# Joining maxima and sums over four partition groups: six VectorE copies in place of a TensorE transpose

## The chip, the cores and the metric

The kernel runs on one core of one Trainium2 chip. The metric is the device time of one execution in microseconds; lower is better. Before the change the median of 3 runs is 2840.31 us (2839.74 to 2840.36). A core has five engines that run their own instruction streams and meet at semaphores: TensorE (PE in the profile, with its weight loads as PEld), VectorE (DVE), ScalarE (ACT), GpSimd (POOL) and SyncE (SP), which issues most transfers. SBUF is the memory that all of them work on; TensorE writes its results to PSUM.

## The reference

One transformer block on 2048 rows of width 576: a modulated layer norm, attention against a cache (32 query heads on 16 key/value heads of width 128, the last 512 keys), and a gated MLP of width 4608. Everything is fp32.

```python
mod = (silu(c) @ w_mod)            # sa, ca, ga, sb, cb, gb
h = layernorm(x) * (1 + ca) + sa
q = (h @ wq)                       # 32 heads of 128
scores = einsum("bhqd,bhkd->bhqk", q, k[last 512]) * 128 ** -0.5
p = softmax(scores)
x = x + ga * (einsum("bhqk,bhkd->bhqd", p, v) @ wo)
h = layernorm(x) * (1 + cb) + sb
x = x + gb * ((relu(h @ W_gate) * (h @ W_up)) @ W_down)
```

## The kernel before

The attention stage runs from about 30 to 1593 us. It is cut into 128 units; a unit u is one query head on one block of 512 queries, against all 512 keys. After it comes the MLP, which the change does not touch. An fp32 product is made of three matmuls: each operand is split into hi (a rounded copy, made by ScalarE) and lo (the rest, made by GpSimd or VectorE), and hi x hi, lo x hi and hi x lo are added up in PSUM.

The order of the work on TensorE, VectorE, ScalarE and GpSimd is written by hand: each engine runs its instructions in the order in which the code issues them. The main loop issues, for unit u:

- the scores s (L541 to L543, 12 matmuls), with keys on partitions and queries along the free axis, and on VectorE t (L546): the maximum over each group of 32 keys, made by a reduction that transposes blocks of 32 x 32;
- `max_pre` (L551): the maximum over the four key tiles, into columns 0 to 15 of the tile mxs. In mxs, partition 32g + j and column b hold the maximum of query 32b + j over the 32 keys of partition group g;
- `sum_pre` (L556): the same for the sums of the unit before, out of its tile ks, into columns 16 to 31;
- `turn` and `spread`: the four partition groups have to be joined. VectorE writes mxs four times over, transposed by blocks of 32, into mt (L562), and TensorE transposes mt into PSUM as qm (L565), after the projection of the next unit (qps, L465, 14 matmuls). Then every partition holds the values of all four groups side by side;
- `max_bc`: VectorE takes the maximum of the four (r, L585), the sum of the four for the unit before (ri, L572), spreads the maxima back along the keys (mb, L589) and inverts the sums (L575);
- p (L602): s - mb on VectorE in two halves, with exp (L604) and hi (L597) on ScalarE; rb (L580), the spread inverse sums; qlo (L523), the low part of the next unit's q, which the next scores need; ks, the sum of the exponentials over the key tiles, begun on VectorE (L619) and finished on GpSimd (L622, two instructions);
- on TensorE the value products pv (L631 to L634) of the unit before and two pieces of the output projection (wo, L687);
- lo (L611) on GpSimd, two halves of 1024 elements, and olo (L676), the low part of an earlier unit's output. Weight splits (L217) for coming units are placed between them.

Scores have two PSUM buffers (psS); projections, qm and pv take turns in two others (psM).

Of the kernel before, what the change touches and what calls it, by code (L numbers as in the profile page):

```python
# [7 lines left out]
F32 = mybir.dt.float32  # L8
# [3 lines left out]
ALU = mybir.AluOpType  # L12
AX = mybir.AxisListType

P = 128
# [11 lines left out]
SUM, MLP0 = 3, 8  # L27
# [4 lines left out]
def kernel(  # L32
# [13 lines left out]
    nc = tc.nc  # L46
# [3 lines left out]
    cp = ctx.enter_context(tc.tile_pool(name="cp", bufs=1))  # L50
# [7 lines left out]
    op = ctx.enter_context(tc.tile_pool(name="op", bufs=3))  # L58
    xp = ctx.enter_context(tc.tile_pool(name="xp", bufs=3))
    sp = ctx.enter_context(tc.tile_pool(name="sp", bufs=2))  # L60
# [4 lines left out]
    psM = psM_scope.__enter__()  # L65
# [3 lines left out]
    ident = cp.tile([P, P], F32, name="ident")  # L69
# [6 lines left out]
    ones = cp.tile([P, P], F32, name="ones")  # L76
    nc.vector.memset(ones, 1.0)

    mxs = cp.tile([P, 32], F32, name="mxs")
    nc.vector.memset(mxs, 0.0)  # L80

    zeros = cp.tile([P, 32], F32, name="zeros")
    nc.vector.memset(zeros, 0.0)
# [217 lines left out]
    def flush(q=None):  # L301
        q = pend if q is None else q
        while q:
            q.pop()()
# [185 lines left out]
    NU = HKV * NQB * 2  # L490
# [17 lines left out]
    def qproj(u, lo, hi):  # L508
        g, qb, h = unit(u)
        if lo == 0:  # L510
            assert ready[qb] == "a"
            ps = psM.tile([P, 512], F32, tag="mm", name=f"qps{u}")
            qst[u] = ps, proj_ops(ps, wqs[h], hT[qb], u)
        for f in qst[u][1][lo:hi]:
            f()

    def q_hi(u):
        qhi[u] = qp.tile([P, 512], F32R, tag="qhi", name=f"qhi{u}")
        nc.scalar.activation(qhi[u], qst[u][0], AF.Copy, bias=0.0, scale=SCALE)  # L519

    def q_lo(u):
        qlo[u] = qp.tile([P, 512], F32R, tag="qlo", name=f"qlo{u}")
        nc.vector.scalar_tensor_tensor(qlo[u], qst.pop(u)[0], SCALE, qhi[u].bitcast(F32),  # L523
                                       op0=ALU.mult, op1=ALU.subtract)

    st_, t4, mt, pt, hi_, lo_, bc, rb, rinv, ks_, pvps, done, o, bps = ({} for _ in range(14))

    def by_sum(u):
        return 0 <= u < SUM
# [3 lines left out]
    def s_half(u, h):  # L533
        g, qb, hd = unit(u)
        k = ks[g]
        t = psS.tile([P, 2, 512], F32, tag="s", name=f"s{u}_{h}")
        st_[u, h] = t
        for j in range(2):
            kt = 2 * h + j
            ps = t[:, j, :]  # L540
            nc.tensor.matmul(ps, k[:, kt, :], qhi[u], start=True, stop=False)  # L541
            nc.tensor.matmul(ps, k[:, 4 + kt, :], qhi[u], start=False, stop=False)  # L542
            nc.tensor.matmul(ps, k[:, kt, :], qlo[u], start=False, stop=True)  # L543
        if h == 0:
            t4[u] = sp.tile([P, 4, 16], F32, tag="t4", name=f"t4_{u}", bufs=1)
        nc.vector.tensor_reduce(t4[u][:, 2 * h:2 * h + 2, :].rearrange("p k b -> p (k b)"),  # L546
                                t.rearrange("p k (b j) -> p (k b) j", j=32),
                                axis=AX.X, op=ALU.max, apply_transpose=True)

    def max_pre(u):  # L550
        nc.vector.tensor_reduce(mxs[:, :16], t4.pop(u).rearrange("p k b -> p b k"), axis=AX.X, op=ALU.max)  # L551

    def sum_pre(u):
        if by_sum(u):
            return
        nc.vector.tensor_reduce(mxs[:, 16:], ks_.pop(u).rearrange("p (b j) -> p b j", j=32),  # L556
                                axis=AX.X, op=ALU.add, apply_transpose=True)

    def turn(u):
        bps[u] = psM.tile([P, 512], F32, tag="mm", name=f"qm{u}")  # L560
        mt[u] = sp.tile([P, P], F32, tag="mt", name=f"mt{u}", bufs=1)
        nc.vector.transpose(mt[u].rearrange("p (a b) -> p a b", a=4), mxs[:, None, :].to_broadcast([P, 4, 32]))  # L562

    def spread(u):
        nc.tensor.transpose(bps[u][:, :P], mt.pop(u), ident)  # L565

    def quads(u, k):
        return bps[u][:, :P].rearrange("p (a k b) -> p k b a", a=4, k=2)[:, k]

    def sum_add(u):  # L570
        r = rinv[u] = sp.tile([P, 16], F32, tag="ri", name=f"ri{u}", bufs=1)
        nc.vector.tensor_reduce(r, quads(u + 1, 1), axis=AX.X, op=ALU.add)  # L572

    def sum_inv(u):
        nc.vector.reciprocal(rinv[u], rinv[u])  # L575

    def sum_bc(u):
        r = rinv.pop(u)
        rb[u] = bp.tile([P, 512], F32, tag="bc", name=f"rb{u}")
        nc.vector.transpose(rb[u].rearrange("p (b j) -> p b j", j=32),  # L580
                            r[:, :, None].to_broadcast([P, 16, 32]))

    def max_bc(u):
        r = sp.tile([P, 16], F32, tag="r", name=f"r{u}", bufs=1)
        nc.vector.tensor_reduce(r, quads(u, 0), axis=AX.X, op=ALU.max)  # L585
        if u > SUM:
            sum_add(u - 1)
        m = bp.tile([P, 512], F32, tag="bc", name=f"mb{u}")
        nc.vector.transpose(m.rearrange("p (b j) -> p b j", j=32),  # L589
                            r[:, :, None].to_broadcast([P, 16, 32]))  # L590
        if u > SUM:
            sum_inv(u - 1)
        bc[u] = m

    def hi_half(u, h):
        hi_[u, h] = pp.tile([P, 2, 512], F32R, tag="hi", name=f"hi{u}_{h}")
        nc.scalar.copy(hi_[u, h], pt[u, h])  # L597
# [11 lines left out]
    def lo_half(u, h):  # L609
        lo_[u, h] = pp.tile([P, 2, 512], F32R, tag="lo", name=f"lo{u}_{h}", bufs=2)  # L610
        nc.gpsimd.tensor_sub(lo_[u, h], pt[u, h], hi_[u, h].bitcast(F32))  # L611
# [54 lines left out]
    def o_mul(u):  # L666
        o[u] = rb.pop(u)
        nc.vector.tensor_tensor(o[u], done.pop(u), o[u], op=ALU.mult)

    def o_hi(u):  # L670
        ohi[u] = op.tile([P, 512], F32R, tag="ohi", name=f"ohi{u}")
        nc.scalar.copy(ohi[u], o[u])

    def o_lo(u):
        olo[u] = op.tile([P, 512], F32R, tag="olo", name=f"olo{u}")
        nc.gpsimd.tensor_sub(olo[u], o.pop(u), ohi[u].bitcast(F32))  # L676
# [45 lines left out]
    def piece(n):  # L722
        add = wo_piece(*pieces[n][1:], seed=seeds.get(n))

        def end():
            add()
            put_seed(n + 1)

        (pend_act if n in seeds else pend).append(end)
        return n in seeds  # L730
# [944 lines left out]
    mlp = mlp_slots()  # L1675

    def last_unit():
        spread(NU)
        sum_add(NU - 1)
        sum_inv(NU - 1)  # L1680
        sum_bc(NU - 1)
        o_mul(NU - 1)
# [67 lines left out]
    def run(u, k):  # L1750
        t = 10 * u + k
        while sched and sched[-1][0] <= t:
            fn, args = sched.pop()[2:]
            fn(*args)
# [11 lines left out]
    for u in range(NU):  # L1766
        run(u, 0)
        if u > 1 and u % 2 == 0:
            o_hi(u - 2)
            o_lo(u - 2)  # L1770
        s_half(u, 0)
        s_half(u, 1)
        max_pre(u)
        if u:
            sum_pre(u - 1)
        turn(u)
        run(u, 1)
        if u + 1 < NU:
            qproj(u + 1, 0, 14)
        else:  # L1780
            piece(at[10 * u + 1])
        if u == 1:
            hi_half(0, 0)
            hi_half(0, 1)
            lo_half(0, 0)
            lo_half(0, 1)
        run(u, 2)
        if u + 1 == NU:
            pv_half(u - 1, 0, True)
        spread(u)  # L1790
        max_bc(u)
        if u + 1 < NU:
            q_hi(u + 1)
        run(u, 3)
        if 10 * u + 3 in at:
            piece(at[10 * u + 3])
        if u > 1 and u % 2:
            o_hi(u - 2)
            o_lo(u - 2)
        run(u, 4)  # L1800
        if by_sum(u - 1):
            pv_sums(u - 1)
        elif u + 1 == NU:
            pv_half(u - 1, 1, True)
        elif u:
            pv_half(u - 1, 0)
        flush(pend_act)
        exp_half(u, 0)
        flush()
        run(u, 5)  # L1810
        if u == 0:
            q_lo(1)
        exp_half(u, 1)
        if u > SUM:
            sum_bc(u - 1)
        if 0 < u < NU - 1:
            q_lo(u + 1)
        if by_sum(u - 1):
            sums_inv(u - 1)
        ksum_op(u, 0)  # L1820
        ksum_op(u, 1)
        run(u, 6)
        if SUM < u < NU - 1:
            pv_half(u - 1, 1)
        if 10 * u + 6 in at:
            piece(at[10 * u + 6])
        run(u, 7)
        if u:
            o_mul(u - 1)
        flush()  # L1830
        run(u, 8)
        if u + 1 == NU:
            flush(pend_act)
        if u:
            hi_half(u, 1)
        flush(pend_act)
        if u:
            lo_half(u, 0)
            lo_half(u, 1)
        run(u, 9)  # L1840
# [56 lines left out]
```

## Time and profile before

| what | before |
|---|---|
| median of 3 runs | 2840.31 us |
| the profiled execution, span of its core | 2839.2 us, 1.1 us under the median of the runs |
| TensorE busy | 2823.0 us (99%) |
| VectorE busy | 2194.6 us (77%) |
| ScalarE busy | 1431.0 us (50%) |
| GpSimd busy | 2206.1 us (78%) |
| granted TensorE clock | 1.000 |

A row of the profile names the engine, the line of the kernel, the operation, the tile written and the tiles read, their shapes and the count. In a list by time the first number is the start in us and the second the duration of the row's instructions together; what stands in brackets is how long the engine was idle before it and which instruction ended that. An instruction's record begins when its engine takes it up, so a wait inside the instruction is part of its duration.

### The profile page before, as it was taken

What the parts mean: (1) busy time and instruction counts of PE and PEld (TensorE: products, weight loads), DVE (VectorE), ACT (ScalarE), POOL (GpSimd) and SP (SyncE); (2) the same over time, 40 slices, a digit from 0 to 9 for tenths busy, and PEclk for the clock granted to TensorE, in tenths of its full rate; (3) what the DMA queues carried; (4) which work ended last, traced back from release to release, by engine and by line L of the source; (5) the groups of instructions that cost most, each with busy time, mean ns of one, the idle gap of its engine ahead of it and who ended that gap; (6) DMA issues with size and microseconds to landing.
All of it is one profiled execution on the core that took longest, in us unless ns stands there. A gap on an engine that the chain in (4) does not pass through costs nothing.

```text
span 2839.2 us, 41692 instructions
## 1 busy us (share of the span) xinstructions
PE 2823.0 (99%) x15183; PEld 2457.3 (87%) x15183; DVE 2194.6 (77%) x3220; ACT 1431.0 (50%) x2020; POOL 2206.1 (78%) x1596
## 2 busy tenths in 40 slices
PE   9999999999999999999999999999999999999999
PEld 7888888888888888888888888888888888888888
DVE  8988788888888888777988877787787566666666
ACT  6766666676666666666756433333333222222220
POOL 6878888888898988777788766778888577777773
PEclk9999999999999999999999999999999999999999
DMA  6322122223332223322244465666677844444443
GB/s 248 109 76 97 60 94 95 84 70 109 106 96 85 93 67 132 100 69 86 73 144 136 149 219 203 228 228 232 248 254 281 313 154 155 156 156 154 152 149 136
DMA packets 166876, 411.40 MB, mean 145 GB/s; under 512 B 15728, under 2 KB 62576, under 8 KB 166672
## 3 DMA queue, kind: packets, MB, share of 16 engines
q1 hardware_dynamic: 132768, 287.65, 31.4%
q10 hardware_dynamic: 33904, 121.09, 10.9%
q8 instruction: 120, 1.97, 0.3%
q14 instruction: 84, 0.69, 0.1%
HBM read 276.53 MB, written 160.73 MB: 154 GB/s over the span
## 4 chain that ended last, share of the span: by engine, by line
PE 90%; POOL 4%; DVE 2%; ACT 2%; issue 1%; DMA 1%; ACTq 0%; SPq 0%; POOLq 0%; DVEq 0%
PE gh_P L1163 28%; PE wo L687 12%; PE qps L465 12%; PE md L687 9%; PE mf L771 6%; PE s L543 4%; PE s L542 4%; PE s L541 3%; PE pv L634 3%; PE pv L632 3%; PE pv L631 3%; POOL lo L611 2%; PE gu L1163 1%; POOL ks L622 1%; ACT p L604 1%
## 5 line engine op out<-in xcount | busy, mean ns | idle before, releaser
L611 POOL TENSOR_TENSOR lo<-p,hi 128x1024 fp32r<-128x1024 f32 x256 | 610.1, 2405 | 0.5
L622 POOL TENSOR_TENSOR ks<-ks,p 128x512 f32<-128x512 f32 x250 | 334.5, 1338 | 247.5 <-ACT p L604 203.4
L546 DVE TRANSPOSE_TENSOR_REDUCE t<-s 128x32 f32<-128x1024 f32 x256 | 317.6, 1245 | 137.9 <-PE s L543 125.6
L1163 PE MATMUL gh_P<-hop_B,wop 128*128 128x512 f32 x1470 | 352.9, 390 | 0.6 <-issue 0.6
L1163 PEld LDWEIGHTS gh_P<-hop_B,wop 128*128 128x128 f32 x1470 | 270.0, 188 | 51.2 <-DVE q L1200 0.8
L602 DVE TENSOR_TENSOR p<-s,mb 128x1024 f32<-128x1024 f32 x256 | 299.9, 1209 | 0.3
L465 PE MATMUL qps<-hTa,wA 128*128 128x512 f32 x1176 | 282.6, 391 | 0.7 <-DVE hTa L447 0.3
L1163 PE MATMUL gh_P<-hop_T,wop 128*128 128x512 f32 x1138 | 282.8, 390 | 0.0
L687 PE MATMUL wo<-woga,ohi 128*128 128x288 f32 x1344 | 279.1, 300 | 1.0 <-POOL woga L217 0.5
L604 ACT ACTIVATE p<-p 128x1024 f32<-128x1024 f32 x256 | 270.4, 1056 | 17.4 <-DVE p L602 17.4
L597 ACT CAST hi<-p 128x1024 fp32r<-128x1024 f32 x256 | 268.9, 1051 | 6.9
L465 PEld LDWEIGHTS qps<-hTa,wA 128*128 128x128 f32 x1176 | 220.1, 188 | 47.9 <-DVE hTa L447 0.8
L687 PE MATMUL md<-wogb,hhi 128*128 128x288 f32 x1280 | 257.2, 294 | 0.0
L519 ACT ACTIVATE qhi<-qps 128x512 fp32r<-128x512 f32 x128 | 76.6, 598 | 337.2 <-PE qps L465 337.2
L1163 PEld LDWEIGHTS gh_P<-hop_T,wop 128*128 128x128 f32 x1138 | 208.8, 188 | 39.3
L687 PEld LDWEIGHTS wo<-woga,ohi 128*128 128x128 f32 x1344 | 218.7, 188 | 16.2 <-ACT p L604 0.8
L687 PEld LDWEIGHTS md<-wogb,hhi 128*128 128x128 f32 x1280 | 212.3, 188 | 10.5 <-DVE q L1188 0.2
L698 DVE TENSOR_TENSOR acc<-md,acc 128x576 f32<-128x576 f32 x160 | 120.0, 754 | 107.2 <-PE md L687 106.1
L1163 PE MATMUL gh_P<-hy_T,wop 128*128 128x512 f32 x618 | 200.6, 391 | 0.0
L687 PE MATMUL wo<-woga,olo 128*128 128x288 f32 x672 | 198.8, 296 | 1.2 <-POOL olo L676 1.1
L687 PE MATMUL md<-wogb,hlo 128*128 128x288 f32 x640 | 188.8, 295 | 0.0
L696 ACT COPY acc<-wo 128x576 f32<-128x576 f32 x228 | 145.0, 636 | 55.1 <-PE wo L687 50.5
(322 smaller groups left out, 7279.7 us busy)
## 6 DMA issues: line engine op xcount, KB each, us to landing
wop<-wk_P SPq DMA_DIRECT2D x133, 640.0 KB
wk_P<-wop ACTq DMA_DIRECT2D x119, 640.0 KB
wr<-wlay SPq DMA_DIRECT2D x68, 384.0 KB
againq<-akq SPq DMA_DIRECT2D x22, 640.0 KB
againo<-ako SPq DMA_DIRECT2D x18, 576.0 KB
rogb<-wd SPq DMA_DIRECT2D x36, 288.0 KB
rwA<-wq SPq DMA_DIRECT2D x32, 320.0 KB
roga<-wo SPq DMA_DIRECT2D x32, 288.0 KB
```

The lines of the kernel that those rows point to most:

```text
L465: return [lambda i=i, a=a, b=b: nc.tensor.matmul(ps, a, b, start=(i == 0), stop=(i == n - 1)) for i, (a, b) in enumerate(ops)]
L546: nc.vector.tensor_reduce(t4[u][:, 2 * h:2 * h + 2, :].rearrange("p k b -> p (k b)"), t.rearrange("p k (b j) -> p (k b) j", j=32), axis=AX ...
L597: nc.scalar.copy(hi_[u, h], pt[u, h])
L602: nc.vector.tensor_tensor(p, t, bc[u][:, None, :].to_broadcast([P, 2, 512]), op=ALU.subtract)
L604: nc.scalar.activation(p, p, AF.Exp, bias=0.0, scale=1.0)
L611: nc.gpsimd.tensor_sub(lo_[u, h], pt[u, h], hi_[u, h].bitcast(F32))
L622: nc.gpsimd.tensor_tensor(ks_[u], ks_[u], p[:, j, :], op=ALU.add)
L687: nc.tensor.matmul(ps[:, half, :H2], a[:, sl], w[b][:, cs], start=(n == 0 and seed is None), stop=(n == 5), skip_group_check=seed is not None)
L696: nc.scalar.copy(av, ps[:, :, :H2])
L698: nc.vector.tensor_tensor(av, ps[:, :, :H2], av, op=ALU.add)
L771: nc.tensor.matmul(ps[:, j, :H2], x[:, sl], w[:, c:c + H2], start=i == 0, stop=i == 2)
L1163: nc.tensor.matmul(ps, a, c, start=s not in ("P2", "P3") and i == 0, stop=i == len(ops) - 1, skip_group_check=True)
```

## The change

The tile mxs gets a second axis of four. After max_pre and sum_pre, three VectorE copies bring the 32 columns of partition groups 1, 2 and 3 beside those of group 0, on partitions 0 to 31. Two reductions there take the maximum and the sum of the four, into the tile both, and three copies bring the result to the partitions of the other groups. The turn on VectorE, the transpose on TensorE and its PSUM tile are gone, and so is the last transpose behind the last unit. `max_bc` reads the maxima, and `sum_inv` the sums, from both.

```diff
-    mxs = cp.tile([P, 32], F32, name="mxs")
+    mxs = cp.tile([P, 4, 32], F32, name="mxs")
     nc.vector.memset(mxs, 0.0)
+    both = cp.tile([P, 32], F32, name="both")
+    nc.vector.memset(both, 0.0)
...
     def turn(u):
-        bps[u] = psM.tile([P, 512], F32, tag="mm", name=f"qm{u}")
-        mt[u] = sp.tile([P, P], F32, tag="mt", name=f"mt{u}", bufs=1)
-        nc.vector.transpose(mt[u].rearrange("p (a b) -> p a b", a=4), mxs[:, None, :].to_broadcast([P, 4, 32]))
-
-    def spread(u):
-        nc.tensor.transpose(bps[u][:, :P], mt.pop(u), ident)
-
-    def quads(u, k):
-        return bps[u][:, :P].rearrange("p (a k b) -> p k b a", a=4, k=2)[:, k]
-
-    def sum_add(u):
+        for q in range(1, 4):
+            nc.vector.tensor_copy(mxs[:32, q, :], mxs[32 * q:32 * q + 32, 0, :])
+        for j, op in ((0, ALU.max), (1, ALU.add)):
+            if u > SUM if j else u < NU:
+                c = slice(16 * j, 16 * j + 16)
+                nc.vector.tensor_reduce(both[:32, c], mxs[:32, :, c].rearrange("p q b -> p b q"),
+                                        axis=AX.X, op=op)
+        for q in range(1, 4):
+            nc.vector.tensor_copy(both[32 * q:32 * q + 32, :], both[:32, :])
+
+    def sum_inv(u):
         r = rinv[u] = sp.tile([P, 16], F32, tag="ri", name=f"ri{u}", bufs=1)
-        nc.vector.tensor_reduce(r, quads(u + 1, 1), axis=AX.X, op=ALU.add)
-
-    def sum_inv(u):
-        nc.vector.reciprocal(rinv[u], rinv[u])
+        nc.vector.reciprocal(r, both[:, 16:])
...
     def max_bc(u):
-        r = sp.tile([P, 16], F32, tag="r", name=f"r{u}", bufs=1)
-        nc.vector.tensor_reduce(r, quads(u, 0), axis=AX.X, op=ALU.max)
-        if u > SUM:
-            sum_add(u - 1)
         m = bp.tile([P, 512], F32, tag="bc", name=f"mb{u}")
         nc.vector.transpose(m.rearrange("p (b j) -> p b j", j=32),
-                            r[:, :, None].to_broadcast([P, 16, 32]))
+                            both[:, :16, None].to_broadcast([P, 16, 32]))
...
     def last_unit():
-        spread(NU)
-        sum_add(NU - 1)
         sum_inv(NU - 1)
...
-        spread(u)
         max_bc(u)
```

VectorE's order in one unit before the change, from max_pre to the sum of the exponentials (a name's number is its allocation; ks is the tile of the unit before):

```order
L551 TENSOR_REDUCE mxs<-t_26_4045 128x16
L556 TENSOR_REDUCE mxs<-ks_3994 128x16
L562 STREAM_TRANSPOSE mt_4058<-mxs 128x128
L585 TENSOR_REDUCE r_4076<-qm_4057 128x16
L572 TENSOR_REDUCE ri_4078<-qm_4057 128x16
L589 STREAM_TRANSPOSE mb_4080<-r_4076 128x512
L575 RECIPROCAL ri_4078<-ri_4078 128x16
L602 TENSOR_TENSOR p_0_4110<-s_0_4038,mb_4080 128x1024
```

The same place on VectorE in the changed kernel, one unit later, with the changed kernel's line numbers:

```order
L553 TENSOR_REDUCE mxs<-t_27_4196 128x16
L558 TENSOR_REDUCE mxs<-ks_4153 128x16
L563 COPY mxs<-mxs 32x32 x3
L567 TENSOR_REDUCE both<-mxs 32x16 x2
L570 COPY both<-both 32x32 x3
L584 STREAM_TRANSPOSE mb_4231<-both 128x512
L574 RECIPROCAL ri_4233<-both 128x16
L597 TENSOR_TENSOR p_0_4269<-s_0_4189,mb_4231 128x1024
```

The turn and the two reductions out of PSUM have made room for three copies, two reductions and three copies, all ahead of mb; nothing else on VectorE has moved.

TensorE's order at the end of the next unit's projection before the change (qps is the projection, wo the piece of the output projection behind it):

```order
L465 MATMUL qps_5448<-hTa_7_1779,wA_4410 128x512
L465 MATMUL qps_5448<-hTa_8_1727,wA_4410 128x512 x2
L565 MATMUL qm_5444<-ident,mt_5445 128x128
L687 MATMUL wo_3_5414<-woga_4914,ohi_5044 128x288 x2
L687 MATMUL wo_3_5414<-woga_4914,olo_5046 128x288
```

And the same place on TensorE in the changed kernel:

```order
L467 MATMUL qps_5492<-hTa_7_1794,wA_4441 128x512
L467 MATMUL qps_5492<-hTa_8_1737,wA_4441 128x512 x2
L682 MATMUL wo_3_5453<-woga_4949,ohi_5080 128x288 x2
L682 MATMUL wo_3_5453<-woga_4949,olo_5082 128x288
L682 MATMUL wo_3_5453<-woga_5274,ohi_5270 128x288 x2
```

The piece of the output projection now follows the projection at once; the order of all other matmuls is what it was. GpSimd, ScalarE and SyncE keep their orders.

More of the change, by code (lines that the diff above doesn't have):

```diff
@@ L524, in q_lo @@
                                        op0=ALU.mult, op1=ALU.subtract)
-    st_, t4, mt, pt, hi_, lo_, bc, rb, rinv, ks_, pvps, done, o, bps = ({} for _ in range(14))
+    st_, t4, pt, hi_, lo_, bc, rb, rinv, ks_, pvps, done, o = ({} for _ in range(12))
     def by_sum(u):
@@ L550, in max_pre @@
     def max_pre(u):
-        nc.vector.tensor_reduce(mxs[:, :16], t4.pop(u).rearrange("p k b -> p b k"), axis=AX.X, op=ALU.max)
+        nc.vector.tensor_reduce(mxs[:, 0, :16], t4.pop(u).rearrange("p k b -> p b k"), axis=AX.X, op=ALU.max)
     def sum_pre(u):
@@ L555, in sum_pre @@
             return
-        nc.vector.tensor_reduce(mxs[:, 16:], ks_.pop(u).rearrange("p (b j) -> p b j", j=32),
+        nc.vector.tensor_reduce(mxs[:, 0, 16:], ks_.pop(u).rearrange("p (b j) -> p b j", j=32),
                                 axis=AX.X, op=ALU.add, apply_transpose=True)
     def turn(u):
-        bps[u] = psM.tile([P, 512], F32, tag="mm", name=f"qm{u}")
-        mt[u] = sp.tile([P, P], F32, tag="mt", name=f"mt{u}", bufs=1)
-        nc.vector.transpose(mt[u].rearrange("p (a b) -> p a b", a=4), mxs[:, None, :].to_broadcast([P, 4, 32]))
-    def spread(u):
-        nc.tensor.transpose(bps[u][:, :P], mt.pop(u), ident)
-    def quads(u, k):
-        return bps[u][:, :P].rearrange("p (a k b) -> p k b a", a=4, k=2)[:, k]
-    def sum_add(u):
+        for q in range(1, 4):
[8 more added lines that the diff above has]
+    def sum_inv(u):
         r = rinv[u] = sp.tile([P, 16], F32, tag="ri", name=f"ri{u}", bufs=1)
-        nc.vector.tensor_reduce(r, quads(u + 1, 1), axis=AX.X, op=ALU.add)
-    def sum_inv(u):
-        nc.vector.reciprocal(rinv[u], rinv[u])
+        nc.vector.reciprocal(r, both[:, 16:])
     def sum_bc(u):
```

## The prediction

> **What bounds the kernel now.** I read the busy times of the attention stage first, then the chain of work that ended last, then one unit of that stage on VectorE and on GpSimd, and last the waits.
>
> The stretches view, columns: span; then PE, PEld, DVE, ACT and POOL busy with their counts; clock; DMA share; GB/s. It is followed by the turn's own group in the same stretch:
>
> ```profile
> 100.00:1575.00 1475.00, 1470.33 (x7746) 1267.54 (x7745) 1232.48 (x1936) 998.63 (x1340) 1232.05 (x761) 1.00 0.29 94
> L562 DVE STREAM_TRANSPOSE mt<-mxs x122: 311/311/314, 105.0 to 1573.4; 128x128 f32<-128x128 f32 x122
> ```
>
> TensorE is busy for 1470.33 of 1475 us at full clock: it is the bound. The 122 turns give 1475/122 = 12.09 us a unit. VectorE and GpSimd are each busy 1232/122 = 10.10 us of that. So either could lose 2 us a unit before it became the bound, if the two stayed independent of each other. Whether they do is the question of this case.
>
> The chain of waits in that unit shows what the removed matmul costs TensorE:
>
> ```profile
> 804.12 0.23 PE s L541
> ...
> 804.58 0.23 PE s L543
> ...
> 806.87 3.19 PE qps L465 x14
> 810.05 0.11 PE qm L565
> 810.16 1.59 PE wo L687 x12
> ```
>
> The transpose holds the chain for 0.11 us. The scores (s) take 806.87 - 804.12 = 2.75 us. Their third matmul, the first that needs qlo, starts 0.46 us after the first.
>
> VectorE in the next unit, from the maxima to the sum of the exponentials:
>
> ```profile
> 805.54 2.61 DVE L546 TRANSPOSE_TENSOR_REDUCE t<-s 128x32 f32<-128x1024 f32 x2 [1.58 <-PE s L543]
> ...
> 809.10 0.31 DVE L562 STREAM_TRANSPOSE mt<-mxs 128x128 f32<-128x128 f32 x1
> 810.20 0.23 DVE L585 TENSOR_REDUCE r<-qm 128x16 f32<-128x64 f32 x1 [0.78 <-PE qm L565]
> 810.34 0.21 DVE L572 TENSOR_REDUCE ri<-qm 128x16 f32<-128x64 f32 x1
> 810.47 0.70 DVE L589 STREAM_TRANSPOSE mb<-r 128x512 f32<-128x512 f32 x1
> ...
> 811.23 2.34 DVE L602 TENSOR_TENSOR p<-s,mb 128x1024 f32<-128x1024 f32 x2
> ...
> 814.10 0.65 DVE L523 SCALAR_TENSOR_TENSOR qlo<-qps,qhi 128x512 fp32r<-128x512 f32 x1
> 814.68 1.15 DVE L619 TENSOR_TENSOR ks<-p 128x512 f32<-128x512 f32 x1
> ```
>
> GpSimd in the same time:
>
> ```profile
> 808.03 4.75 POOL L611 TENSOR_TENSOR lo<-p,hi 128x1024 fp32r<-128x1024 f32 x2
> 812.75 1.29 POOL L217 TENSOR_TENSOR kv<-rkv,kv 128x512 fp32r<-128x512 f32 x1
> 814.00 1.28 POOL L676 TENSOR_TENSOR olo<-rb,ohi 128x512 fp32r<-128x512 f32 x1
> 816.27 2.75 POOL L622 TENSOR_TENSOR ks<-ks,p 128x512 f32<-128x512 f32 x2 [0.99 <-ACT p L604]
> ```
>
> The turn starts at 809.10, about 1 us into a closed GpSimd run: each instruction begins before the one ahead has ended (812.75 against 808.03 + 4.75), and the run ends only at 815.28. Today this costs nothing: the turn and its reductions do not care what GpSimd does (L562 above never leaves 311 to 314 ns).
>
> **Removed.** 129 PE transposes at 0.11 us are 14.2 us of the bound. TensorE also waits for the turn now and then, and VectorE waits for the transpose in nearly every unit (columns: total us, times, longest):
>
> ```profile
> PEld qm L565 <- DVE mt L562: 6.9, 11, 1.0
> DVE r L585 <- PE qm L565: 92.0, 121, 1.3
> ```
>
> So at best 14 + 7 = 21 us go from TensorE. The PSUM slot that each transpose took is freed too; I count that as nothing, because the 4.7 us that TensorE is not busy in the stage already hold every wait for a slot.
>
> **Added, as bare durations.** Six fp32 copies, SBUF to SBUF; the two reductions stay, on SBUF and 32 partitions. The nearest row for a copy is this one, and GpSimd was idle beside it (its next instruction started at 320.68):
>
> ```profile
> 320.29 0.18 DVE L162 COPY macc<-macc 128x64 f32<-128x64 f32 x1
> 320.68 2.67 POOL L622 TENSOR_TENSOR ks<-ks,p 128x512 f32<-128x512 f32 x2 [1.50 <-ACT p L604]
> ```
>
> Independent small instructions follow each other 0.13 us apart (810.20, 810.34, 810.47) and a dependent one waits for the whole of the one before. I estimate 0.3 us for three copies, 0.4 for two reductions, 0.35 for three copies: 1.05 us. If nothing overlapped it would be 6 x 0.18 + 0.44 = 1.5 us. The present stretch from turn to mb is 810.47 - 809.10 = 1.37 us. So by durations the edit is a draw on VectorE (-0.3 to +0.15 us a unit, covered by the 1.58 us idle before t), and the 14 to 21 us would be the whole effect.
>
> **Added, as a wait.** The copies are a kind of instruction that this stage hardly holds: one source, source and destination both in SBUF. The rows nearest to them with GpSimd at work are a tiny TENSOR_SCALAR of that kind and a two-input TENSOR_TENSOR in the MLP, each with GpSimd's rows around it:
>
> ```profile
> 73.88 0.73 DVE L353 TENSOR_SCALAR rsa<-mva 128x4 f32<-128x4 f32 x1
> 71.92 2.68 POOL L622 TENSOR_TENSOR ks<-ks,p 128x512 f32<-128x512 f32 x2 [2.22 <-DVE ks L619]
> ```
>
> ```profile
> 1641.95 4.16 DVE L952 TENSOR_TENSOR ws<-wr,wr 128x768 f32<-128x768 f32 x1
> 1640.67 1.43 POOL L217 TENSOR_TENSOR wogb<-rogb,wogb 128x576 fp32r<-128x576 f32 x1
> 1642.07 1.28 POOL L1179 TENSOR_TENSOR hlo<-c,hhi 128x512 fp32r<-128x512 f32 x1
> 1643.32 0.73 POOL L923 TENSOR_TENSOR wop<-wr,wop 32x256 fp32r<-32x256 f32 x1
> 1644.02 1.28 POOL L924 TENSOR_TENSOR wop<-wr,wop 128x512 fp32r<-128x512 f32 x1
> ```
>
> L353 works on 4 elements and takes 0.73 us: it ends at 74.61, when the GpSimd ks has ended (74.60). L952 starts at 1641.95 and ends at 1646.11, 0.81 us after GpSimd's closed run ends at 1645.30. It did not get in at 1642.10, 1643.35 or 1644.05, where one GpSimd instruction followed another without a gap. So VectorE instructions of these kinds stand still until GpSimd pauses. I take the copies to be of the same kind, because a copy is nearest to L353: one input, fp32, SBUF to SBUF. No row shows a COPY beside a busy GpSimd; the two ends are no wait at all, and a wait for the end of the run.
>
> The Trainium skill speaks against the change here: SBUF — State Buffer, section "Who interferes with whom", says that copy, cast and tensor_scalar can enter a mode that takes the port pair which VectorE shares with GpSimd, and that one of the two then blocks completely. The trace agrees for tensor_scalar (0.73 us on 4 elements); for a copy no run here shows it yet.
>
> **The new period, with the wait.** Let G be the end of GpSimd's run, when the first copy gets through.
>
> - mb starts at G + 1.05, and p 811.23 - 810.47 = 0.76 later, G + 1.8. Its first half ends at G + 3.0.
> - ScalarE then runs exp, hi, exp in this order, each 1.05 us by the rows below: G + 6.2.
> - VectorE's own ks starts 814.68 - 811.23 = 3.45 us after p and, undisturbed, ends by G + 6. So GpSimd's next ks starts at G + 6.25. Until then GpSimd has nothing to do: all of its earlier work ended at G.
> - qlo ends 3.52 us after p starts, G + 5.3, and the third score matmul waits for it. The scores end 2.3 us later (2.75 - 0.46) at G + 7.6, the two t at about G + 9, max and sum about 1 us after (809.10 against 805.54 + 2.61) at G + 10: the next copies are issued.
> - GpSimd's ks ends at G + 8.95 and lo follows at once. The copies meet a run that goes on until GpSimd has done its whole 10.10 us of the unit: G + 16.35.
>
> ```profile
> 813.09 1.06 ACT L604 ACTIVATE p<-p 128x1024 f32<-128x1024 f32 x1
> 814.18 1.05 ACT L597 CAST hi<-p 128x1024 fp32r<-128x1024 f32 x1
> ```
>
> So the two engines, which now overlap, take turns: 6.25 + 10.10 = 16.35 us a unit against 12.09. TensorE no longer bounds the stage, and its 14 us return nothing. 122 units by 4.26 us are +520 us on the profiled 2839.2 us: 3359. I leave the first five units out (they wait for loads), and take 10 us off for runs that break early. The median, 2840.31 us, lies 1.1 us above this span, for what goes on around it: **3350 us**. Own range 3230 to 3430: about a fifth of the runs broken early, or some copies caught a second time.
>
> **Rivals.**
>
> *A, the wait ends at the first boundary.* If a waiting copy is let in when the GpSimd instruction under way ends, three copies go between the two lo (G + 8.95 + 2.4 = 11.35), the reductions run beside the second lo, and the last three copies follow it at 13.95 (11.35 + 0.25 + 2.37). p then starts at about 15.1 in place of G + 1.8: a period of 13.3, +1.2 us by 122 = +150, 2990 us. L952, which passed three boundaries, speaks against it; for it, that copies are far shorter. The same rule is what the Trainium skill's SBUF page says in that section: the pair is held for one instruction, by whichever came first; its run-long wait in L952 is more than that. In between lie runs that break after the lo: 8.95 + 4.75 = 13.7 us, +1.6 us, 3036 us.
>
> *B, copies never wait.* Then the durations decide: 2840.3 - 14.2 = 2826 us, to 2819 us if TensorE's waits for the turn go too. For it: L562, L585 and L572 ignore GpSimd. Against: L353.
>
> *C, no change.* The copies wait now and then, and the wait just eats the 14 us: +0.12 us a unit beyond the slack. The qlo row leaves 816.53 - 814.75 = 1.78 us of slack (s's third matmul against qlo's end):
>
> ```profile
> 816.53 0.23 PE s L543
> ```
>
> A wait below about 2 us would be hidden, but the closed run leaves 815.28 - 809.10 = 6.2 us.
>
> **How the numbers follow.** Forecast 0.55, A with its middle ground 0.27, B 0.15, C 0.03. The range has to hold the first two: from 2980 to 3440 us. This kernel's measurement tells a difference of 0.2% from none. Faster is B, 0.15; same is C, 0.03; slower is the rest, 0.82.
>
> **What would show it.** In the changed profile the first copy of each unit should have a mean of microseconds, where the other five are near 0.1 to 0.2, and it should end within 0.05 us of the end of a GpSimd run. GpSimd's idle time ahead of ks (L622) should grow from 2 us to about 6 a unit; TensorE should wait about 4 us a unit, for qlo, ahead of s L543; attention should end near 2100 us; the MLP after it should be unchanged. If a copy takes 0.2 us beside a running lo, step "added, as a wait" is wrong and B holds; if copies end at the boundary between the two lo, A does.

## The result and the profile after

The changed kernel takes 3382.77 us (median of 5 runs, 3380.77 to 3383.77) against 2840.31 us: a ratio of 1.191, 95% interval 1.1895 to 1.1924. The forecast was slower, 3350 us, in a range of 2980 to 3440.

The stretches view of the changed kernel, over the attention stage (same columns as in the prediction), and the copies in of the same stretch:

```profile
100.00:2115.00 2015.00, 1672.05 (x7710) 1369.20 (x7708) 1881.80 (x2578) 1018.12 (x1356) 1245.74 (x769) 0.91 0.21 70
L563 DVE COPY mxs<-mxs x369: 168/1242/7112, 109.8 to 2115.0; 32x32 f32<-32x32 f32 x185
```

369 copies are 123 units in 2015 us: 16.38 us a unit, against 12.09 before. GpSimd does the same work as before, 1245.74/123 = 10.13 us a unit, and now idles 6.25 us of each. VectorE looks 93% busy, but a good part of that is standing: a copy in of 32 x 32 elements takes 0.168 us at the least, 1.242 in the median and 7.112 at the most. Over the whole kernel, with the columns count, busy time in us and mean in ns of one:

```profile
L563 DVE COPY mxs<-mxs 32x32 f32<-32x32 f32 x387 | 528.0, 1364 | 7.9
L570 DVE COPY both<-both 32x32 f32<-32x32 f32 x387 | 128.6, 332 | 7.9
```

The 774 copies take 656.6 us together; at 0.17 us each they would take 132. TensorE is the bound no longer: it idles 343 us of the stage, where it idled 4.7.

One unit on VectorE, each copy in shown by itself:

```profile
1066.16 0.71 DVE L558 TRANSPOSE_TENSOR_REDUCE mxs<-ks 128x16 f32<-128x512 f32 x1
1066.90 0.69 DVE L563 COPY mxs<-mxs 32x32 f32<-32x32 f32 x1
1067.61 2.35 DVE L563 COPY mxs<-mxs 32x32 f32<-32x32 f32 x1
1069.97 1.24 DVE L563 COPY mxs<-mxs 32x32 f32<-32x32 f32 x1
1071.24 0.43 DVE L567 TENSOR_REDUCE both<-mxs 32x16 f32<-32x64 f32 x2
1071.71 0.54 DVE L570 COPY both<-both 32x32 f32<-32x32 f32 x3
1072.28 0.71 DVE L584 STREAM_TRANSPOSE mb<-both 128x512 f32<-128x512 f32 x1
...
1073.05 2.33 DVE L597 TENSOR_TENSOR p<-s,mb 128x1024 f32<-128x1024 f32 x2
...
1075.92 0.65 DVE L525 SCALAR_TENSOR_TENSOR qlo<-qps,qhi 128x512 fp32r<-128x512 f32 x1
```

GpSimd at the same time, the two halves of lo by themselves:

```profile
1065.17 2.39 POOL L606 TENSOR_TENSOR lo<-p,hi 128x1024 fp32r<-128x1024 f32 x1
1067.53 2.39 POOL L606 TENSOR_TENSOR lo<-p,hi 128x1024 fp32r<-128x1024 f32 x1
1069.88 1.29 POOL L671 TENSOR_TENSOR olo<-rb,ohi 128x512 fp32r<-128x512 f32 x1
1077.52 2.67 POOL L617 TENSOR_TENSOR ks<-ks,p 128x512 f32<-128x512 f32 x2 [6.35 <-ACT p L599]
```

Lay the two side by side. The first copy ends at 1067.59, when the first lo has ended (1067.56). The second ends at 1069.96, when the second lo has ended (1069.92). The third ends at 1071.21, when olo has ended (1071.17). Three copies, three GpSimd instructions, each let through 0.03 to 0.04 us after an end. Then GpSimd has nothing left, the copies out run in 0.54 us for three, and GpSimd waits 6.35 us for the exponentials.

Other units follow the same rule. Of the 774 copies of the kernel 367 take more than 0.3 us (287 in and 80 out), and 355 of these end 0.03 to 0.04 us after the first end of a GpSimd instruction that they meet. The other 12 are taken up in the last section.

TensorE's idle time in the same place and the totals of the waits view (us, times, longest):

```profile
1060.23 0.79 PE L545 MATMUL s<-qlo,kv 128*128 128x512 f32 x1 [1.10 <-DVE qlo L525]
...
1074.31 0.50 PE L543 MATMUL s<-qhi,kv 128*128 128x512 f32 x1 [0.57 <-DVE p L597]
...
1076.63 0.50 PE L545 MATMUL s<-qlo,kv 128*128 128x512 f32 x1 [1.59 <-DVE qlo L525]
```

```profile
POOL ks L617 <- ACT p L599: 660.4, 113, 8.3
...
PEld s L545 <- DVE qlo L525: 207.8, 109, 3.0
PE s L545 <- DVE qlo L525: 158.0, 104, 2.5
...
PEld s L543 <- DVE p L597: 143.5, 87, 3.5
```

The scores wait for VectorE twice, once for p, which frees their PSUM, and once for qlo. The idle time of TensorE, 343 us in 123 units, is 2.8 us a unit. After attention nothing has changed: from VectorE's first L952 (L947 in the changed kernel) to the end of the span it is 1234.4 us before (from 1604.81) and 1233.8 now (from 2147.16).

### The profile page after: what moved, and what is told of

Its sections match the earlier page's. It is cut to its first block, busy times and chain, and to the rows that moved or that the text cites. A ratio compares the mean times of both kernels' runs of the same rounds, so it can differ in the third digit from the quotient of the medians.

```text
span 3381.0 us, 41961 instructions
## 1 busy us (share of the span) xinstructions
PE 3013.8 (89%) x15054; PEld 2549.6 (75%) x15054; DVE 2860.8 (85%) x3866; ACT 1437.7 (43%) x2020; POOL 2203.3 (65%) x1596
## 4 chain that ended last, share of the span: by engine, by line
PE 43%; DVE 19%; issue 1%; ACT 0%; DMA 0%; SPq 0%; DVEq 0%; ACTq 0%
PE gh_P L1158 23%; PE md L682 8%; DVE mxs L563 7%; PE mf L766 5%; DVE p L597 3%; DVE t L548 2%; PE s L545 2%; DVE both L570 1%; PE s L543 1%; PE s L544 1%; PE wo L682 1%; DVE mxs L558 1%; DVE mb L584 1%; DVE rb L579 1%; DVE qlo L525 1%
## 5 line engine op out<-in xcount | busy, mean ns | idle before, releaser
L563 DVE COPY mxs<-mxs 32x32 f32<-32x32 f32 x387 | 528.0, 1364 | 7.9
L467 PE MATMUL qps<-hTa,wA 128*128 128x512 f32 x1176 | 292.4, 400 | 5.0 <-DVE hTa L443 4.5
L467 PEld LDWEIGHTS qps<-hTa,wA 128*128 128x128 f32 x1176 | 230.8, 197 | 58.7 <-DVE hTa L443 4.9
L545 PE MATMUL s<-qlo,kv 128*128 128x512 f32 x336 | 175.3, 522 | 110.3 <-DVE qlo L525 110.3
L543 PE MATMUL s<-qhi,kv 128*128 128x512 f32 x336 | 170.7, 508 | 100.8 <-DVE p L597 100.1
L682 PEld LDWEIGHTS wo<-woga,ohi 128*128 128x128 f32 x1344 | 227.2, 191 | 34.0 <-DVE hTa L449 19.4
L545 PEld LDWEIGHTS s<-qlo,kv 128*128 128x128 f32 x336 | 82.9, 247 | 163.3 <-DVE qlo L525 145.8
```

The source lines that it names most:

```text
L467: return [lambda i=i, a=a, b=b: nc.tensor.matmul(ps, a, b, start=(i == 0), stop=(i == n - 1)) for i, (a, b) in enumerate(ops)]
L563: nc.vector.tensor_copy(mxs[:32, q, :], mxs[32 * q:32 * q + 32, 0, :])
L682: nc.tensor.matmul(ps[:, half, :H2], a[:, sl], w[b][:, cs], start=(n == 0 and seed is None), stop=(n == 5), skip_group_check=seed is not None)
```

## The experiments

Two things had to be told apart first: whether the copies wait for GpSimd at all, or whether moving data between partition groups is slow by itself; and then what a copy waits for, the end of GpSimd's closed run (as forecast) or the end of one instruction. A closed run is a row of GpSimd instructions that follow one another without a gap, and a boundary is the place where one of them ends and the next begins. Where a time has no interval it is one execution, next to 2840 us for the kernel before on the same chip. Line numbers are those of the changed kernel unless an edit shifts them.

### The same moves without a copy

```diff
-            nc.vector.tensor_copy(mxs[:32, q, :], mxs[32 * q:32 * q + 32, 0, :])
+            nc.vector.tensor_reduce(mxs[:32, q, :], mxs[32 * q:32 * q + 32, 0, :, None], axis=AX.X, op=ALU.max)
...
-            nc.vector.tensor_copy(both[32 * q:32 * q + 32, :], both[:32, :])
+            nc.vector.tensor_reduce(both[32 * q:32 * q + 32, :], both[:32, :, None], axis=AX.X, op=ALU.max)
```

> The six moves are made by TENSOR_REDUCE over an axis of length one (a maximum of a single element) in place of COPY: same data, same partitions, same order. The theory that a COPY waits for a pause of GpSimd: a reduction does not wait (the two joining reductions took 0.24 to 0.27 us throughout), so the stage falls back to TensorE's pace without the transposes: 2815 to 2830 us, below the kernel before. The rival that moving data between partition groups on VectorE is slow by itself, or that the chain of dependent small instructions is: it stays above 3300 us.

Measured: 2851.2 us (5 runs, 2850.3 to 2853.3), 1.0038 of the kernel before (1.0024 to 1.0052). The two groups of moves, and one unit on VectorE:

```profile
L563 DVE TENSOR_REDUCE mxs<-mxs x387: 174/175/179, 30.7 to 1605.3; 32x32 f32<-32x32 f32 x194
L570 DVE TENSOR_REDUCE both<-both x387: 175/177/182, 31.6 to 1606.1; 32x32 f32<-32x32 f32 x194
```

```profile
710.16 0.71 DVE L558 TRANSPOSE_TENSOR_REDUCE mxs<-ks 128x16 f32<-128x512 f32 x1
710.90 0.55 DVE L563 TENSOR_REDUCE mxs<-mxs 32x32 f32<-32x32 f32 x3
711.48 0.44 DVE L567 TENSOR_REDUCE both<-mxs 32x16 f32<-32x64 f32 x2
711.96 0.56 DVE L570 TENSOR_REDUCE both<-both 32x32 f32<-32x32 f32 x3
712.55 0.71 DVE L584 STREAM_TRANSPOSE mb<-both 128x512 f32<-128x512 f32 x1
```

532 of the 542 us are gone with another kind of instruction for the same data. The slowest of the 774 moves takes 0.182 us, GpSimd busy or not. So the loss is the wait of the copies. But the kernel is 11 us slower than the one with the transpose, not 14 to 21 faster, although TensorE has 129 matmuls less: the expectation missed on that side. The stretch from the first move to mb is 712.55 - 710.90 = 1.65 us, where turn, transpose and reductions took 1.37. The stage on the four engines:

```profile
100.00:1587.00 1487.00, 1469.93 (x7661) 1264.37 (x7660) 1373.75 (x2559) 1004.37 (x1345) 1240.92 (x764) 1.00 0.29 94
```

VectorE is busy 92% of the stage where it was 84%, and TensorE idles 17.1 us where it idled 4.7. The waits view of this kernel, TensorE's weight loads from 100 to 1570 us, begins with the value products, which wait for GpSimd's lo; the same row stood at 5.2 us in 12 times before:

```profile
PEld pv L629 <- POOL lo L606: 14.5, 30, 1.1
```

Later p on VectorE makes ks and lo later on GpSimd, and lo was the input that came nearest to late already. That is part of the loss: from the seventh to the 128th turn (104.99 to 1573.42 us before, 112.15 to 1585.54 here) TensorE's busy time falls by 6.8 us and its idle time grows by 11.7, 5 us in all. The other 7.2 us are lost ahead of the seventh turn; from 30 to 100 us VectorE was busy 92% of the time already before the change, which leaves little to hide a longer stretch in. No run took these first units apart.

### Only one side as copies

Moves in by reductions, moves out by copies:

> Only the three moves into group 0 are made by TENSOR_REDUCE; the three back out stay COPY. Waiting theory: the first copy out meets the same GpSimd run, about 0.7 us further in, and takes over the whole wait; the stretch from the pause to GpSimd's next ks gets about 0.65 us shorter, so 122 x 0.65 = 80 us less than the changed kernel: about 3300 us. Rival (each copy has a price of its own): half of the loss goes, about 3110 us.

Moves in by copies, moves out by reductions:

> Only the three moves back out are made by TENSOR_REDUCE; the three in stay COPY. Waiting theory: the first copy in waits as before, and only the few second catches of the copies out fall away: 3330 to 3385 us. Rival (each copy has a price of its own): about 3110 us.

Measured: 3246.0 us and 3332.9 us. The copies that are left, columns busy time and mean in ns of one:

```profile
L570 DVE COPY both<-both 32x32 f32<-32x32 f32 x387 | 472.9, 1222 | 7.9
```

```profile
L563 DVE COPY mxs<-mxs 32x32 f32<-32x32 f32 x387 | 540.3, 1396 | 7.9
```

In either kernel three copies are left and a mean of 1.2 to 1.4 us on each. The copies out, 0.18 us each in the changed kernel's unit above, take over nearly the whole wait as soon as the copies in are not there to take it. So the wait is not a price per copy; it hangs on what GpSimd is doing. That speaks for both forms of the waiting theory; the first run came 54 us under its expectation.

### Copies that cannot wait, copies that can

Four copies in of 33 elements; the destination of a copy is either one run or three rows of 11 with one element between the rows. All else is the same, the moves out are reductions. The diff is that of the split rows; in the control the last size of quad is 11, so that the rows touch.

```diff
+    quad = cp.tile([P, 4, 3, 12], F32, name="quad")
...
-            nc.vector.tensor_copy(mxs[:32, q, :], mxs[32 * q:32 * q + 32, 0, :])
+            nc.vector.tensor_copy(quad[:32, q, :, :11], mxs[32 * q:32 * q + 32, :].rearrange("p (a b) -> p a b", a=3))
```

> Four copies in (group 0 too) of 33 elements, one run to one run; the joining reductions become four over parts of the 33 columns, the moves out are TENSOR_REDUCE. A control for the next kernel. Waiting theory: as the changed kernel with its copies out made by reductions, plus some 0.3 us a unit for more instructions: 3340 to 3420 us.

> The same instructions and elements as the control, but the destination of each copy is three rows of 11 with a gap of one element between them, the source one run of 33. If every COPY from SBUF to SBUF waits for GpSimd: the same time as the control. If only copies wait whose access can be halved and streamed over two ports (the Trainium skill, VectorE: DVE Perf Modes, section What auto-detection actually checks, asks that the outermost counts be both even or equal; here they are 33 and 3): the copies do not wait, 2820 to 2850 us.

Measured: 3419.4 us for the control and 2865.6 us for the split rows. The copies of the two, minimum, median and maximum in ns; the control first:

```profile
L565 DVE COPY quad<-mxs x516: 169/1228/7060, 30.5 to 2169.2; 32x33 f32<-32x33 f32 x172
```

```profile
L565 DVE COPY quad<-mxs x516: 174/175/181, 29.9 to 1617.7; 32x33 f32<-32x33 f32 x172
```

The same instruction with the same elements between the same partitions takes 0.175 us always, or waits for microseconds; one element of gap decides. Of the 516 copies into split rows 511 begin while a GpSimd instruction is under way, and none waits. The time of the split rows is 16 us above the expected range. In the trace the waiting copy has source and destination as one run of 33, the other a source of 33 and a destination of 11 by 3. By the Trainium skill, VectorE: DVE Perf Modes, section "What auto-detection actually checks", a copy inside SBUF uses two ports if the outermost counts are both even or equal. These runs agree, in so far as the copy of 33 to 33 waits and the copy of 33 to 3 rows never does. The form that waits is 0.005 us shorter at its best, 0.169 us against 0.174.

### Less work on GpSimd

The copies stay; GpSimd's olo, or its lo, is left out, and TensorE reads ohi or hi in its place.

```diff
-        nc.gpsimd.tensor_sub(olo[u], o.pop(u), ohi[u].bitcast(F32))
+        olo[u] = ohi[u]
...
-        nc.gpsimd.tensor_sub(lo_[u, h], pt[u, h], hi_[u, h].bitcast(F32))
+        lo_[u, h] = hi_[u, h]
```

> The changed kernel without GpSimd's olo (L671): TensorE uses ohi in its place, so the low part of the attention output is left out of the projection; everything else is kept. Waiting theory: GpSimd's run is 1.30 us shorter in each of 122 units and VectorE waits as much less: 3383 - 159 = about 3225 us. Rival (the copies or their chain are slow by themselves): no change, 3383 us, since GpSimd has idle time.

> The changed kernel without GpSimd's lo (L606): TensorE uses hi in its place, so the low part of the exponentials is left out of the value product; everything else is kept. Waiting theory: GpSimd's work falls from 10.1 to 5.3 us a unit, 6.25 + 5.3 = 11.55 us is less than TensorE's 12.0, and TensorE is the bound again: 2815 to 2860 us. Rival (the copies or their chain are slow by themselves): 3383 us as it is.

> The kernel before without GpSimd's lo, with the same work left out. Both theories: TensorE is the bound and GpSimd has idle time, so no change: 2830 to 2842 us. If it fell by hundreds of us, the run without lo would say nothing on the copies.

Measured: 3280.4 us without olo, 2870.3 us without lo, and 2830.3 us for the kernel before without lo. Taking away GpSimd's work, which is on nobody's path in the kernel before (-10 us), gives the changed kernel 512 us back. The copies without lo:

```profile
L563 DVE COPY mxs<-mxs x387: 169/172/1807, 30.8 to 1622.6; 32x32 f32<-32x32 f32 x194
```

Most now find GpSimd idle (median 0.172 us). The run without lo ended 10 us above the expected range. Without olo the gain is 102 us where 159 was expected. A shorter run did not return its whole length, and why was not looked into. It does not tell the two forms of the waiting theory apart, since in 127 of 129 turns GpSimd stands idle after the last copy, as in the changed kernel.

### One copy, two copies

The first one or two of the three moves in are copies; the other moves are reductions. The diff is that of one copy; for two the limit is 2.

```diff
-            nc.vector.tensor_copy(mxs[:32, q, :], mxs[32 * q:32 * q + 32, 0, :])
+            if q <= 1:
+                nc.vector.tensor_copy(mxs[:32, q, :], mxs[32 * q:32 * q + 32, 0, :])
+            else:
+                nc.vector.tensor_reduce(mxs[:32, q, :], mxs[32 * q:32 * q + 32, 0, :, None], axis=AX.X, op=ALU.max)
```

> One of the six moves (the first in) is a COPY, the other five are TENSOR_REDUCE. Theory as forecast (a copy stands until GpSimd's closed run ends): the one copy waits as long as the three did, 3280 to 3340 us. Theory from the changed kernel's trace (a copy is let in when the GpSimd instruction under way ends, and the next GpSimd instruction goes ahead of the next copy): it waits for the rest of one lo, 1.3 us or so, and p starts at G + 13.5 in place of G + 16.3 or later, a period of 11.7 us, which TensorE covers: 2850 to 2920 us.

> Two of the six moves (the first two in) are COPY. Theory as forecast (wait for the end of the run): 3300 to 3340 us, as with three. One copy at each boundary: the second passes when the second lo ends, G + 13.75, p starts at G + 15.7, a period of 13.9 us: 2840 + 122 x 1.75 = about 3050 us.

Measured: 2981.7 us with one and 3213.4 us with two. The copies of the first and of the second kernel:

```profile
L564 DVE COPY mxs<-mxs x129: 169/1125/7122, 30.3 to 1732.0; 32x32 f32<-32x32 f32 x129
```

```profile
L564 DVE COPY mxs<-mxs x258: 169/1578/7114, 30.1 to 1964.2; 32x32 f32<-32x32 f32 x129
```

| copies in a unit | us |
|---|---|
| none (all moves are reductions) | 2851.2 |
| 1 in | 2981.7 |
| 2 in | 3213.4 |
| 3 in | 3332.9 |
| 3 in and 3 out (the change) | 3382.8 |

If a copy stood until the run had ended, one would cost as much as three, and the forecast's theory expected 3280 to 3340 us for it. It costs 131 us; the second adds 232, the third 119. That is the order of the unit above: the rest of one lo, a whole lo (2.39 us), an olo (1.29 us). Spread over 128 units the steps are 1.0, 1.8 and 0.9 us, smaller than these, since not every copy meets an instruction that has just begun. A waiting copy is let in when the GpSimd instruction under way ends, and GpSimd's next one is let in ahead of the next copy. Both runs lie above their expected figure (by 62 us above the range, by 163): the boundary rule has the order right and my sums with it were too small. The traces show the rule directly: GpSimd stands idle after the last copy of a unit in 19 of 129 turns with one copy, in 28 with two, in 80 with three in, and in 127 with all six. With few copies VectorE goes on while GpSimd's run is still under way.

### The copies on ScalarE

```diff
-            nc.vector.tensor_copy(both[32 * q:32 * q + 32, :], both[:32, :])
+            nc.scalar.copy(both[32 * q:32 * q + 32, :], both[:32, :])
```

All six on ScalarE, and then only the three out (as in the diff), with reductions in:

> All six copies on ScalarE, the rest as in the changed kernel. Waiting theory: ScalarE does not share what the copies on VectorE wait for, so no wait of microseconds appears; VectorE loses about 1.1 us of work a unit against the kernel with reductions, but the way over ScalarE and back adds an estimated 0.5 us to the stretch ahead of mb, of which 1.1 us of idle time ahead of t covers all: 2820 to 2850 us. Rival (data cannot be moved between partition groups cheaply in the middle of this chain by any engine): above 2900 us.

> The moves in by TENSOR_REDUCE on VectorE, the three copies out on ScalarE: half of the kernel before this one, one way over ScalarE in place of two. Waiting theory: no wait for GpSimd; VectorE has about 0.55 us less work a unit than with all six as reductions (2851 us): 2825 to 2850 us.

Measured: 2899.2 us, 1.0204 (1.0187 to 1.0221), and 2887.4 us, 1.0166 (1.0151 to 1.0181). Both missed their ranges upwards. Groups of the kernel with all six; the last number is the engine's idle time before them:

```profile
L570 ACT COPY both<-both 32x32 f32<-32x32 f32 x387 | 83.8, 216 | 66.5 <-DVE both L567 63.5
L563 ACT COPY mxs<-mxs 32x32 f32<-32x32 f32 x387 | 83.7, 216 | 284.1 <-DVE mxs L558 272.1 <-DVE mxs L553 8.9
```

No copy waits for GpSimd on ScalarE. But VectorE stands 0.74 us for each way over it (three copies of 0.22 us), and ScalarE itself stands 272 us waiting for the sums, with its other work of the unit queued behind. Which of the two costs the 36 to 48 us over the reductions was not separated. No kernel with the transpose taken out was faster than the kernel before.

## Why the prediction was right, and where it was not

**What bounds the kernel, and what the removed matmul is worth:** right on the bound. The 14 us never came back in the changed kernel, since TensorE was no longer the bound. Their size stays open: in the kernel with reductions TensorE's busy time fell by 6.8 us over 121 turns, where 0.11 us each gives 13.3.

**Bare durations ("a draw on VectorE"):** mis-sized. Three small moves take 0.55 us, not 0.3, because they follow each other 0.19 us apart and not 0.13; the stretch is 1.65 us by reductions, above the bound of 1.5. And 0.28 us more did not hide: 2851 us where the rival without a wait gave 2817 to 2826. The cover I named, the idle time ahead of t, is not the only one that matters: by the waits view, pv waits for lo first, and lo hangs on p through GpSimd's queue. Of the 11 us lost there 7.2 fall in the first units, which the forecast left out of its sums.

**The wait:** right that copies wait for GpSimd, read from a TENSOR_SCALAR of four elements. Wrong in what they wait for. The forecast read the run of L952, a TENSOR_TENSOR with two inputs that passed three boundaries, and took copies to behave the same. They get in at a boundary, one at a time. The row was one of two sorts, and the kernel before held the other sort too:

```profile
1677.25 1.99 DVE L952 TENSOR_TENSOR ws<-wr,wr 128x768 f32<-128x768 f32 x1
1677.14 1.29 POOL L1179 TENSOR_TENSOR hlo<-c,hhi 128x512 fp32r<-128x512 f32 x1 [0.68 <-ACT hhi L1178]
1678.39 1.44 POOL L923 TENSOR_TENSOR wop<-wr,wop 32x256 fp32r<-32x256 f32 x1
1679.80 1.28 POOL L924 TENSOR_TENSOR wop<-wr,wop 128x512 fp32r<-128x512 f32 x1
```

Here L952 ends at 1679.24, 0.81 us after L1179's end at 1678.43: it got in at the first boundary, and L923, 0.73 us in the forecast's rows, took 1.44. Of the 29 rows of L952 that begin while a GpSimd instruction runs with another behind it without a gap, seven got in at the first boundary, and 22 passed at least one. In all of the 22, and in none of the seven, an instruction on 32 partitions (L923) had begun earlier in the same closed run. The forecast made a rule of one row of the second sort.

The Trainium skill's rule quoted in the prediction (SBUF — State Buffer, section "Who interferes with whom": the pair is held for one instruction) is what most copies showed. The first sign listed, one long copy and five short ones, appeared in 19 of 128 units only.

**The new period:** 16.35 us forecast, 16.38 measured; GpSimd's idle time 6.25 forecast, 6.25 measured. The number is right by way of a wrong step, and that is luck: six copies let in one by one outlast GpSimd's run in 127 of 129 turns, so waiting several times for one instruction and waiting once for the run come to the same. With one or two copies the forecast's step would have been wrong by 300 and 100 us. The sign for TensorE did not come as listed: it idles 2.8 us a unit and not 4, for p as well as for qlo, and its own work grew from 12.05 to 13.59 us a unit at a granted clock of 0.91 (1470.33/122 and 1672.05/123).

The 33 us that the forecast is short are not in the period but at its edges. At the seventh turn the changed kernel is 24.6 us behind (129.63 against 104.99): the first units, left out because they wait for loads, lost too. The 121 turns after it lose 513 us (2111.51 against 1573.42 at the 128th), and the last one 3. The 10 us taken off for early breaks had no ground.

**Rival A** had the rule that holds and the wrong price: it let three copies through one boundary and came to 2990 us, about what one copy gives (2982). **Rival B** fell: wherever copies of one run to one run were left beside a busy GpSimd, they waited. **Rival C** fell with the period.

## What to carry to other kernels

Before a VectorE instruction moves into a chain on the critical path, look for its kind (inputs, both ends in SBUF) beside a busy GpSimd in the trace: a duration that jumps to the end of a GpSimd instruction is a wait, whatever the engine's busy share says. Look at all rows of the kind: here one row out of 29 was taken for the rule. Price such an instruction by the GpSimd instruction that it will meet, and several in a row by as many GpSimd instructions, not by their own 0.17 us. The same data went through without waiting as a reduction over an axis of one element, or as a copy whose source and destination have unequal odd outer counts.

## What the runs showed that was not expected

A few copies did stand through several boundaries: the longest in the changed kernel took 7.112 us, the one copy of the kernel with one copy 7.122 at most, with a median of 1.125. One such unit of the changed kernel, GpSimd and then VectorE:

```profile
1080.14 0.45 POOL L1092 TENSOR_TENSOR wb_P<-wa_P,wb_P 32x128 fp32r<-32x128 f32 x1
1080.56 0.73 POOL L1094 TENSOR_TENSOR wa_P<-wa_P,wb_P 128x256 fp32r<-128x256 f32 x1
1081.26 4.73 POOL L606 TENSOR_TENSOR lo<-p,hi 128x1024 fp32r<-128x1024 f32 x2
1085.96 1.28 POOL L219 TENSOR_TENSOR kv<-rkv,kv 128x512 fp32r<-128x512 f32 x1
1087.21 1.28 POOL L671 TENSOR_TENSOR olo<-rb,ohi 128x512 fp32r<-128x512 f32 x1
1081.46 7.06 DVE L563 COPY mxs<-mxs 32x32 f32<-32x32 f32 x1
```

The copy ends at 1088.52, when the run has ended (1088.49). What sets these apart can be read from the traces. Nine first copies of the changed kernel stood through three or four boundaries, and in these nine units, and in no other, GpSimd's split L1092 on 32 partitions runs ahead of lo in the same closed run. It is the same nine units in the kernels with one, two and three copies in. Two copies out that begin beside L1092 pass its end as well, and the last of the 12 began 0.006 us before an end. It is the same sort as the forecast's row of L952. So the forecast's rule, a wait for the end of the run, is what these nine units show; why an instruction on 32 partitions should bring it about was not tried and stays open.

TensorE's granted clock in the stage fell from 1.00 to 0.91. Around one wait, the scores that begin after it and the stretches view show how it goes:

```profile
1057.91 0.80 PE L543 MATMUL s<-qhi,kv 128*128 128x512 f32 x1 [3.15 <-DVE p L597]
```

```profile
1057.00:1064.00 7.00, 4.99 (x11) 3.50 (x12) 5.62 (x7) 5.80 (x7) 2.86 (x3) 0.53 0.00 0
1064.00:1075.00 11.00, 10.43 (x55) 8.62 (x53) 10.08 (x15) 3.12 (x5) 7.17 (x4) 0.99 0.15 41
```

The scores at 1057.91 begin after TensorE has idled 3.15 us, and the granted clock up to 1064 is 0.53. The score matmul at 1060.23, the first after a wait, takes 0.79 us; the one at 1076.63, also the first after a wait, takes 0.50, and in the kernel before most take 0.39. By the Trainium skill, TensorE: Matmul & The Clock Gate, section "What's actually happening", an idle array falls back to half its clock; the 0.53 agrees. TensorE waits for VectorE in those units anyway, so what this adds to the time was not measured.
